# Decayed attention feeding a GELU MLP on one core: loads two chunks further ahead, and group 2's attention visits moved to later MLP blocks

## The chip, the cores and the metric

One core of a Trainium2 chip. The time is device microseconds of one execution of the kernel. Besides the timed runs, one execution is recorded by the hardware profiler; its span (first to last instruction) is shorter than its time by what lies before and after.

## The reference

q, k and v are `[4, 8, 768, 64]` float32 (batch, head, position, head dimension). The attention is causal with a decay `lam` per head and no softmax. Cut to what matters (D is the causal mask of decay powers, and the kernel uses blocks of 128 positions for the same result):

```
for each block of positions:
    intra  = ((qb @ kb.T) * D) @ vb
    inter  = (qb * lam_pow) @ kv_state
    out    = intra + inter
    kv_state = lam_block * kv_state + (kb * rev_pow).T @ vb
x = out as [3072, 512]
result = gelu(x @ w_in) @ w_out        # w_in 512 x 2048, w_out 2048 x 512, exact GELU
```

## The kernel before, in words

**Tiling.** The 3072 tokens are cut into 24 chunks of 128 positions. Chunk n belongs to batch n % 4 and to position block n // 4. Four chunks with the same position block form a group: group g holds chunks 4g to 4g+3, and there are six groups, 0 to 5. For a group the MLP runs as a list of blocks on TensorE (`mlp_blocks`): 16 blocks of `x @ w_in` (L263, four matmuls each, then a GELU on ScalarE at L265), then the blocks of `g @ w_out` (L275, four matmuls each; an output tile of 128 tokens is finished every fourth block, copied by ScalarE at L280 and written by SP at L281). In a middle group that makes 32 blocks.

**Interleaving.** The attention of group g+1 is done between the MLP blocks of group g. The dictionary `visits` says which function runs ahead of block i of group g. For chunks 8 and later, a chunk goes through these steps:

- `load` (L64 to L66): three DMAs issued by GpSimd (POOL), one each for k, q and v, from float32 in DRAM to bf16 in SBUF. Each name has a pool of 12 tiles.
- `request` (L366): `dma_transposes` (L184). SP transposes k into kT by a DMA (L188); POOL multiplies q by the decay powers into `q_hat` (L189); SP transposes `q_hat` into qT by a DMA (L190).
- `decay_k` (L165): POOL multiplies k by decay powers into `k_dec` (L169).
- `pair_a` (L411): `scores` of two chunks on TensorE, kT against qT (L197), then VectorE masks them (L201).
- `quad_b` (L415): `inter` and `intra` of the four chunks on TensorE (L224, L230), then VectorE copies the result to `x_t` (L236), the MLP's next input.
- `kv` (L378): the state update of four chunks (L209 on TensorE, L216 and L217 on VectorE).

**Who sets the order.** Each engine runs its own instructions strictly in the order in which the program issued them. The visits therefore fix the order on POOL and SP, but not the time: POOL and SP run ahead of TensorE as far as their semaphores let them. `requests(n)` is POOL's and SP's part for two chunks: two `request`, two `decay_k`, and last the loads of chunks to come (`prefetch`, L372, which issues every load not yet issued up to its argument). So on POOL the products of one pair, then six loads, then the products of the next pair follow one another. `first_requests` (L383) does chunks 8 and 9 and loads 10 and 11.

**The visits concerned.** For the groups 1 to 4 the block numbers stand in one line (L435), `a0` and `a1` for the two `pair_a`, `b` for `quad_b`, `st` for `kv`:

```
for g in range(1, NG - 1):
    n = (g + 1) * M
    a0, a1, b, st = (10, 21, 26, 31) if g == 1 else (4, 11, 18, 25)
    if g == 1:
        add(g, a0 - 2, lambda n=n: requests(n + 2))
    add(g, a0, lambda n=n: pair_a(n))
    add(g, a1, lambda n=n: pair_a(n + 2))
    if g + 2 < NG:
        add(g, a1 + 1, lambda n=n: requests(n + M))
        add(g, b + 1, lambda n=n: requests(n + M + 2))
```

Group 1 therefore requests chunks 10 and 11 (block 8), 12 and 13 (block 22), and 14 and 15 (block 27). Group 2 visits TensorE with the pairs 12, 13 (block 4) and 14, 15 (block 11), and requests 16, 17 (block 12) and 18, 19 (block 19).

Of the kernel before, what the change touches and what calls it, by code (L numbers as in the profile page):

```python
# [15 lines left out]
def kernel(  # L16
# [23 lines left out]
    M = B  # L40
# [23 lines left out]
    def load(n, name):  # L64
        raw[n, name] = qkv_pool.tile([128, H, D], BF16, tag=name, name=f"{name}_t")
        nc.gpsimd.dma_start(raw[n, name], chunk_of(name, n))  # L66
# [98 lines left out]
    def decay_k(c, eng):  # L165

        if c.so < NB - 1:
            c.k_dec = work_pool.tile([128, H, D], BF16, tag="kd", name="k_dec", bufs=8)
            eng.tensor_mul(c.k_dec, c.k, lam_m[:, :, None].to_broadcast((128, H, D)))  # L169
# [196 lines left out]
    def request(n):  # L366
        begin(n)
        dma_transposes(live[n])
# [3 lines left out]
    def prefetch(upto):  # L372
        while next_load[0] <= min(upto, NCH - 1):
            for name in "kqv":
                load(next_load[0], name)
            next_load[0] += 1

    def kv(*ns):  # L378
        for n in ns:
            next_state(live[n])  # L380
            take_state(live[n])
# [29 lines left out]
    def pair_a(n):  # L411
        for c in (live[n], live[n + 1]):
            scores(c)

    def quad_b(n):  # L415
        quad = [live[n + i] for i in range(M)]
        for c in quad:
            inter(c)
        for c in quad:
            intra(c)  # L420

    def requests(n):
        for m in (n, n + 1):
            request(m)
        for m in (n, n + 1):
            decay_k(live[m], nc.gpsimd)
        prefetch(n + 3)

    def add(g, i, f):
        visits.setdefault((g, i), []).append(f)  # L430


    for g in range(1, NG - 1):
        n = (g + 1) * M
        a0, a1, b, st = (10, 21, 26, 31) if g == 1 else (4, 11, 18, 25)  # L435
        if g == 1:
            add(g, a0 - 2, lambda n=n: requests(n + 2))
        add(g, a0, lambda n=n: pair_a(n))
# [4 lines that stand above are left out]
        add(g, b, lambda n=n: quad_b(n))  # L443
        add(g, st, lambda n=n: kv(n, n + 1, n + 2, n + 3))
# [37 lines left out]
```

## Time and profile before

| what | value |
|---|---|
| median of 6 runs | 215.26 us (213.48 to 218.02) |
| profiled execution | 216.23 us, its span 214.4 us |
| PE (TensorE matmuls) busy | 204.2 us, 95% of the span |
| POOL busy | 101.8 us, all of it ahead of 144 us |
| ACT, DVE busy | 87.2 us, 76.1 us |
| TensorE clock granted | 0.999 |
| k, q and v loads | 71 DMAs by POOL, median 5.2 to 5.9 us from issue to landing |
| kT and qT transposes | 16 and 16 DMAs by SP, median 4.7 and 3.1 us to landing |

A row of the timeline or of the chain gives a start, a duration, an engine with a line of the kernel, and what was written from what; brackets at its end give the idle time before it and what ended it. POOL and SP rows with DMA in them are the issue of a transfer; its landing is given apart, by the view of one tile ("DMA to landing"). Groups of MLP blocks are recognised by their lines: L263 for the first half, L275 for the second. By the stretches of TensorE's timeline, group 2 begins at 86.65 us, group 3 at 120.6, group 4 at 152.5 and group 5 at 183.5.

### The profile page before, as it was taken

To read this page: it belongs to the slowest core of one execution; us is meant where nothing else is said; L and a number is where in the kernel's file an instruction comes from. 1 tells how busy PE (TensorE), PEld (TensorE's weight loads), DVE (VectorE), ACT (ScalarE), POOL (GpSimd) and SP (SyncE) were. 2 spreads that over 40 slices of the span, in tenths; PEclk is the share of its full clock that TensorE was granted. 3 is DMA by queue.
4 is the path that set the end of the run, shared out by engine and by line. 5 is a ranking of instruction groups with operands and counts; after the bars stand their busy time and mean duration, and the time that the engine had idled before them with its cause. 6 is when DMAs were issued, how large, how long until landed. Compare 5 with 4: busy or idle time off the path is not lost.

```text
span 214.4 us, 3549 instructions
## 1 busy us (share of the span) xinstructions
PE 204.2 (95%) x1450; PEld 105.2 (49%) x1474; DVE 76.1 (35%) x122; ACT 87.2 (41%) x153; POOL 101.8 (47%) x117
## 2 busy tenths in 40 slices
PE   7997999999999999996999999999999999999994
PEld 2543654456654465443545444645444644444442
DVE  3777040164393234944046344037244130000000
ACT  5662654325656211553311356312365312566121
POOL 7992433792996965939697684930000000000000
PEclk9999999999999999999999999999999999999999
DMA  8999999999999699996979999993200012100112
GB/s 86 139 145 190 206 207 187 154 213 140 171 88 121 72 154 119 124 146 139 151 98 126 113 243 143 127 151 117 98 0 0 3 49 87 59 3 0 49 49 98
DMA packets 100271, 24.48 MB, mean 114 GB/s; under 512 B 92960, under 2 KB 97312, under 8 KB 100256
## 3 DMA queue, kind: packets, MB, share of 16 engines
q0 software_dynamic: 78064, 13.51, 84.3%
q1 hardware_dynamic: 22192, 10.76, 25.8%
q8 instruction: 11, 0.18, 0.4%
q14 instruction: 4, 0.03, 0.1%
HBM read 27.27 MB, written 6.29 MB: 156 GB/s over the span
## 4 chain that ended last, share of the span: by engine, by line
PE 52%; POOL 20%; DMA 20%; issue 7%; ACT 0%; POOLq 0%
PE o_ps L275 24%; PE h_ps L263 21%; DMA w_out_t<-in_moe_w_out_dram 9%; DMA q_t<-in_q_dram 6%; POOL k_dec L169 5%; POOL k_t L66 5%; POOL q_t L66 4%; DMA w_in_t<-in_moe_w_in_dram 4%; POOL v_t L66 4%; POOL q_hat L189 2%; PE o_ps L289 2%; PE o_ps L230 1%; PE o_ps L224 1%; PE sc_ps L197 1%; DMA qT<-q_hat 1%
## 5 line engine op out<-in xcount | busy, mean ns | idle before, releaser
L263 PE MATMUL h_ps<-x_t,w_in_t 128*128 128x512 bf16 (+2 forms) x422 | 86.0, 355 | 1.9 <-DMA w_in_t<-in_moe_w_in_dram 1.3
L275 PE MATMUL o_ps<-w_out_t,g_t 128*128 128x512 bf16 x356 | 81.1, 379 | 1.3 <-issue 1.0
L265 ACT ACTIVATE g_t<-h_ps 128x512 bf16<-128x512 f32 (+1 forms) x99 | 57.8, 584 | 38.3 <-PE h_ps L263 38.1
L263 PEld LDWEIGHTS <-w_in_t 128*128 128x128 bf16 x432 | 39.3, 98 | 43.1 <-DMA w_in_t<-in_moe_w_in_dram 2.2
L275 PEld LDWEIGHTS <-g_t 128*128 128x128 bf16 x368 | 35.1, 98 | 40.9
L280 ACT COPY o_sb<-o_ps 128x512 f32<-128x512 f32 x23 | 13.5, 586 | 72.6 <-PE o_ps L275 69.7
L201 DVE TENSOR_TENSOR sc_m<-sc_ps,dmask 128x512 bf16<-128x512 f32 x48 | 30.1, 683 | 35.5 <-PE sc_ps L197 35.5
L189 POOL TENSOR_TENSOR q_hat<-q_t,lam_p 128x512 bf16<-128x512 bf16 x16 | 16.8, 1052 | 24.8 <-DMA q_t<-in_q_dram 13.6
L66 POOL DMA_DIRECT2D k_t<-in_k_dram x24 | 22.0, 918 | 6.8 <-DMA w_in_t<-in_moe_w_in_dram 4.3
L66 POOL DMA_DIRECT2D q_t<-in_q_dram x24 | 21.6, 898 | 3.4 <-DMA w_out_t<-in_moe_w_out_dram 3.3
L66 POOL DMA_DIRECT2D v_t<-in_v_dram x23 | 20.8, 905 | 4.0 <-DMA w_out_t<-in_moe_w_out_dram 1.7
L236 DVE CAST x_t<-o_ps 128x512 bf16<-128x512 f32 x16 | 9.9, 684 | 19.9 <-PE o_ps L230 19.9
L169 POOL TENSOR_TENSOR k_dec<-k_t,lam_m 128x512 bf16<-128x512 bf16 x16 | 16.4, 1050 | 0.0
L216 DVE TENSOR_TENSOR tmp<-kv_ps,state 128x512 f32<-128x512 f32 x16 | 10.9, 684 | 15.0 <-PE kv_ps L209 15.0
L324 PE MATMUL idle_ps<-idle 128*128 128x512 bf16 x32 | 11.2, 465 | 1.2 <-DVE idle L105 1.2
L217 DVE TENSOR_TENSOR state<-tmp,lam_blk 128x512 bf16<-128x512 f32 x16 | 12.1, 756 | 0.6
L182 DVE TENSOR_TENSOR qT<-t_ps,lam_q 128x512 bf16<-128x512 bf16 x8 | 5.5, 691 | 14.5 <-PE t_ps L176 14.3
L197 PE MATMUL sc_ps<-qT,kT 64*128 64x128 bf16 x192 | 8.2, 217 | 2.5 <-DMA qT<-q_hat 1.8
L197 PEld LDWEIGHTS <-kT 64*128 64x128 bf16 x192 | 5.7, 94 | 8.1 <-issue 5.3
L230 PE MATMUL o_ps<-sc_m,v_t 128*64 128x128 bf16 x192 | 7.9, 222 | 0.2
L230 PEld LDWEIGHTS <-v_t 128*64 128x64 bf16 x192 | 5.8, 109 | 2.8 <-issue 1.6
L181 ACT COPY kT<-t_ps 128x512 bf16<-128x512 bf16 x8 | 4.7, 586 | 4.7 <-PE t_ps L176 4.7
(41 smaller groups left out, 70.1 us busy)
## 6 DMA issues: line engine op xcount, KB each, us to landing
out_dram<-o_sb SPq DMA_DIRECT2D x23, 256.0 KB, 2.2
k_t<-in_k_dram POOLq DMA_DIRECT2D x24, 128.0 KB, 5.2
q_t<-in_q_dram POOLq DMA_DIRECT2D x24, 128.0 KB, 5.9
v_t<-in_v_dram POOLq DMA_DIRECT2D x23, 128.0 KB, 5.8
w_in_t<-in_moe_w_in_dram POOLq DMA_DIRECT2D x4, 512.0 KB, 11.3
w_out_t<-in_moe_w_out_dram POOLq DMA_DIRECT2D x4, 512.0 KB, 18.2
v_f<-in_v_dram SPq DMA_DIRECT2D x1, 256.0 KB, 3.5
kT<-k_t SPq DMA_TRANSPOSE x16, 4.7
```

The costliest lines, as they stand in the source:

```text
L66: nc.gpsimd.dma_start(raw[n, name], chunk_of(name, n))
L169: eng.tensor_mul(c.k_dec, c.k, lam_m[:, :, None].to_broadcast((128, H, D)))
L189: nc.gpsimd.tensor_mul(q_hat, c.q, lam_p[:, :, None].to_broadcast((128, H, D)))
L197: nc.tensor.matmul(sc_ps[hi][:, hp, :], c.kT[p, hp, :], c.qT[p, hp, :], start=True, stop=True)
L201: nc.vector.tensor_mul(c.sc_m[:, :, hi, :], sc_ps[hi], dmask_r[:, :, hi, :])
L217: nc.vector.tensor_mul(new, tmp, lam_blk)
L230: nc.tensor.matmul(c.o_ps[hi * D:(hi + 1) * D, hp, :], c.v[:, 2 * hp + hi, :], c.sc_m[:, hp, hi, :], start=(c.so == 0 and hp == 0), stop=T ...
L263: nc.tensor.matmul(h_ps[:, f, :], w, x_t[:, ki, lo:hi], start=(ki == 0 and f == 0), stop=(ki == NK1 - 1), skip_group_check=True)
L265: nc.scalar.activation(g_t[:, kf:kf + n_kf, lo:hi], h_ps, ACT.Gelu)
L275: nc.tensor.matmul(om[io], g_t[:, kf, io * C:(io + 1) * C], w_out_t[:, kf, :], start=(kf == 0), stop=(kf == NK2 - 1))
L280: nc.scalar.copy(o_sb, om[io])
L324: nc.tensor.matmul(idle_ps[0], idle[:, :128], idle, start=True, stop=True)
```

## The change

Two edits. In `requests`, the loads at the end go two chunks further, with one exception: the first call (n = 10) goes one further. And group 2 gets visit numbers of its own.

```
@@ requests(n)
         for m in (n, n + 1):
             decay_k(live[m], nc.gpsimd)
-        prefetch(n + 3)
+        prefetch(n + (4 if n == 2 * M + 2 else 5))
@@ visits of the groups 1 to 4
         n = (g + 1) * M
-        a0, a1, b, st = (10, 21, 26, 31) if g == 1 else (4, 11, 18, 25)
+        a0, a1, b, st = {1: (10, 21, 26, 31), 2: (5, 15, 21, 27)}.get(g, (4, 11, 18, 25))
```

What each call of `requests` loads:

| call | before | after |
|---|---|---|
| chunks 10, 11 | 12, 13 | 12, 13, 14 |
| chunks 12, 13 | 14, 15 | 15, 16, 17 |
| chunks 14, 15 | 16, 17 | 18, 19 |
| chunks 16, 17 | 18, 19 | 20, 21 |
| chunks 18, 19 | 20, 21 | 22, 23 |
| chunks 20, 21 | 22, 23 | none |
| chunks 22, 23 | none | none |

In group 2, `pair_a(12)` moves from block 4 to 5, `pair_a(14)` from 11 to 15, `requests(16)` from 12 to 16, `quad_b(12)` from 18 to 21, `requests(18)` from 19 to 22 and `kv` from 25 to 27. The number of instructions on the engines is the same. The order of PE, DVE and POOL changes as told; on SP the write of group 2's first output tile comes ahead of the transposes of chunks 18 and 19 instead of after them.

More of the change, by code (lines that the diff above doesn't have):

```diff
@@ L426, in requests @@
             decay_k(live[m], nc.gpsimd)
-        prefetch(n + 3)
+        prefetch(n + (4 if n == 2 * M + 2 else 5))
     def add(g, i, f):
@@ L434 @@
         n = (g + 1) * M
-        a0, a1, b, st = (10, 21, 26, 31) if g == 1 else (4, 11, 18, 25)
+        a0, a1, b, st = {1: (10, 21, 26, 31), 2: (5, 15, 21, 27)}.get(g, (4, 11, 18, 25))
         if g == 1:
```

## The prediction

> **What bounds the kernel now.** I read part 1 of the page, the waits of PE, the timeline of PE, then POOL's and SP's timelines with the landing of single DMAs. PE is busy for 204.2 of 214.4 us. Its waits name one long stop after the start-up; the others that the view names (0.2 to 1.3 us) lie in the start-up or between two matmuls:
>
> ```profile
> PE sc_ps L197 <- DMA qT<-q_hat: 1.8, 1, 1.8
> ```
>
> PE's timeline shows where it is. Columns: start, length, engine, line, what, and in brackets the idle time before it.
>
> ```profile
> 97.10 0.40 PE L197 MATMUL sc_ps<-qT,kT 64*128 64x128 bf16 x8
> 99.29 0.40 PE L197 MATMUL sc_ps<-qT,kT 64*128 64x128 bf16 x8 [1.79 <-DMA qT<-q_hat]
> ```
>
> This is pair_a(14) at block 11 of group 2: chunk 14's scores ran, chunk 15's waited for its qT. Undisturbed pairs take 0.55 us on the chain; this one ended at 97.10 + 0.55 + 1.97 = 99.62. The stages agree: busy time by windows gives group 2 (86.7 to 120.6) 33.9 us and group 3 (120.6 to 152.5) 31.9 us for 222 matmuls each. So the place holds 1.97 us and no more; all later MLP groups are limited by TensorE's own work.
>
> Why is qT(15) late? POOL's timeline:
>
> ```profile
> 83.84 2.04 POOL L169 TENSOR_TENSOR k_dec<-k_t,lam_m 128x512 bf16<-128x512 bf16 x2
> 85.83 0.94 POOL L66 DMA_DIRECT2D k_t<-in_k_dram  x1
> 86.77 0.88 POOL L66 DMA_DIRECT2D q_t<-in_q_dram  x1
> 87.63 0.91 POOL L66 DMA_DIRECT2D v_t<-in_v_dram  x1
> 88.51 0.90 POOL L66 DMA_DIRECT2D k_t<-in_k_dram  x1
> 89.38 0.91 POOL L66 DMA_DIRECT2D q_t<-in_q_dram  x1
> 90.24 0.92 POOL L66 DMA_DIRECT2D v_t<-in_v_dram  x1
> 91.31 1.04 POOL L189 TENSOR_TENSOR q_hat<-q_t,lam_p 128x512 bf16<-128x512 bf16 x1
> 95.67 1.04 POOL L189 TENSOR_TENSOR q_hat<-q_t,lam_p 128x512 bf16<-128x512 bf16 x1 [3.32 <-DMA q_t<-in_q_dram]
> ```
>
> Six loads (chunks 14, 15) are issued, and the next instruction is a product that needs them. q(15), issued at 89.38, lands 6.2 us later; POOL stands 3.32 us for it. Then SP issues the transpose at 96.74, and by the view of that one tile it lands after
>
> ```profile
> DMA to landing us min/median/max: 2.4/2.4/2.4
> ```
>
> that is at 99.16. The same loads-then-wait repeats for each pair (the bracket of chunk 13's q_hat at 82.84 says 3.50).
>
> **What the Trainium skill says.** "Perfetto Trace Analysis", section "DMA Instruction — SWDGE (GPSIMD)": the recorded end of a GpSimd-issued DMA is the end of writing descriptors, not of moving data. The trace agrees: 0.88 to 0.94 us a row, and from 72 us on 3.4 to 7.9 us to landing. "DMA: Bandwidth & Descriptors", section "Issuing engines are not separate DMA queues": DMAs of SP and GpSimd run on the same 16 engines and interleave. The trace agrees: with kT(12) in flight, v(12) lands at 79.1 and k(13) at 81.8, 2.7 us apart, where loads by themselves land 0.9 apart (k16 to q17: 103.7, 104.5, 105.4, 106.2, 106.9). Same page, section "Queues, rings and completion order": an engine alternates between the queues that have work, packet by packet, which would let a transpose through soon. The trace shows less than that: kT(12), issued at 75.74 behind five loads, lands at 82.8, together with q(13), the last load issued before it; kT(14), qT(16) and qT(18) also land within 0.9 us of the last load ahead. I therefore reckon a transpose as landing behind every load issued before it, and never under 2.4 us.
>
> **The change part by part.**
>
> *Loads 14 moved into the first call.* POOL's burst at 72.17 becomes nine loads at 0.885 each, (91.14 − 85.83)/6: it ends at 80.1, not 77.5. Behind it on POOL stands q_hat(12), at 80.2 instead of 78.30; SP's qT(12) goes from 79.37 to 81.3, kT(13) behind it to 82.6, and qT(13), which still waits for q(13) at 82.8 and q_hat(13), stays at about 83.9. But v(14) is now ahead of these transposes and lands at 84.5 (v13) plus three loads, about 87.5 to 88; the transposes follow at about 0.55 us each (kT18, qT18, kT19: 120.0, 120.7, 121.2), so qT(13) lands at about 89.5 instead of 86.4. Its user, pair_a(12) at block 5, comes at 90.40 + 0.86 = 91.26. Cost: nothing, hidden by some 1.8 us; if the landing takes 7 us as kT(12) did, still 0.3 us of cover.
>
> *Nine loads (15, 16, 17) in the second call.* Issued from 85.9 to 93.8. In the built program each load waits on a semaphore shared with the load eight before it; for v(17), the last, that is k(15), due near 90 and wanted at 92.9: no stall. q_hat(14) starts at 93.95 (before 91.31), q_hat(15) directly after it at 95.0 (before 95.67), since q(15), now second of the nine, is there by about 92. POOL's 3.32 us wait is gone and 2.65 us of load issues have taken its place. On SP the order is fixed: qT(14) at 95.0, kT(15) at 96.3, qT(15) at 97.6 (1.3 apart, as at 105.68, 106.96, 108.28). So **qT(15) is issued 0.9 us later than before**; what was gained on q(15) SP's queue gives back. And it is no longer alone: loads 16 and 17 are ahead of it. The six bursts from 72 to 144 us, first to last landing, take 8.8, 6.7, 4.6, 6.7, 5.1 and 5.4 us for five intervals each, 1.24 us a load with their transposes included. From v(13) at 84.5, twelve loads give v(17) at 99.4, and three transposes at 0.55 give qT(15) at 101.05.
>
> *The later visit.* pair_a(14) at block 15 comes four blocks later than 97.10; a block is 13.82/16 = 0.864 us (group 5's L263 stretch, 183.48 to 197.30), so it starts at 100.56 and wants qT(15) at 100.84. It starts 0.13 after the landing (99.16 to 99.29), at 101.18: a stall of 0.35.
>
> *What follows.* quad_b at block 21 starts 6 blocks after block 15, 106.1 or a little later; sc_m of the pair takes 2.5 us and is done by 104. kv at block 27 is at about 113.2, and needs the score banks that the copy to x_t gives back by 111. Its VectorE work (5.5 us, as 114.16 to 119.7) ends near 119.2; pair_a(16) takes those banks at about 122. Loads 18 to 23 are earlier than before, whose users had no wait already. Tiles suffice: the loads of chunk 20 take those of chunk 8, done with at the kv of group 1 (86 us). kT(18) now stands behind an output write of SP, at about 106; it is wanted past 128. All at no cost.
>
> *Sum:* −1.97 + 0.35 = −1.62. Span 214.4 − 1.6 = 212.8, profiled execution 216.23 − 1.6 = 214.6. The median is 0.97 below the profiled execution: 213.6, 0.75% faster.
>
> **The rivals.**
>
> *The stall only moves (half or less of the gain).* qT(15) lands between 101.7 and 102.7 since loads and transposes run at burst 2's and 4's rate (6.7/5 = 1.34 us): v(17) at 100.6, qT(15) at 102.2, stall 1.5, net −0.5: 214.8. For it: two of the six bursts. Against: 16 loads in a row landed from 40.6 to 54.6 at 0.93 us each.
>
> *Slower: the queue of loads becomes the bound.* One mechanism: a transpose waits out all loads ahead of it, and there are always some now. It decides against the change when qT(15) lands after 102.7, that is when the twelve loads take over 1.38 us each. At burst 1's 8.8/5 = 1.76 they end at 105.6, qT(15) at 107.3, stall 6.6, net +4.6; halfway, at 1.5, net +1.5, 216.7. For it: burst 1 is the place where the change puts more loads, and one write of outputs and three transposes fall between. Against: that burst had the output write in its first interval (k12 to q12, 2.5 us).
>
> *It does nothing to the ordinary run.* The profiled run is slower than the median, and the fastest, 213.48, is 2.75 us below it: the 1.97 may be smaller elsewhere. Then 215.0.
>
> **How the numbers follow.** Forecast (gain of 1 us or more) 0.58: 213.6. Stall moves 0.2: 214.8. Does nothing 0.08: 215.0. Slower 0.14: 216.7. The range reaches from 212.4 (the whole 1.97 plus a sampling of 0.9 us, the runs being spread over 4.5) to 216.4, most of the slower case; the likeliest case alone has 213.0 to 214.3. A measurement of this kernel can tell about 1% from no change, 2.15 us. The gain cannot be over 1.97, so faster by over 1% needs luck in the sampling: 0.15. Slower by over 1% is the upper half of the slower case: 0.08. Within: 0.77.
>
> **What would show it.** Group 2 in 32 to 32.4 us; PE's stop at L197 gone or under 0.5 us and no new one at pair_a(12); nine loads in a row on POOL twice; no bracket on the q_hat of chunk 15; qT(13) landing near 89.5, qT(15) issued near 97.6 and landing near 101. I am wrong if qT(15) lands past 102, if a load waits for the one eight before it and holds q_hat(14) back, or if PE stops near 91.

## The result, and the profile after

The changed kernel took 215.52 us (median of 36 runs, 213.28 to 218.92) against 214.85 us (73 runs) of the kernel before. The ratio is 1.0021 with a 95% interval of 1.0004 to 1.0037, taken over undisturbed runs alone, which leaves out six of the changed kernel with a granted clock of 0.991 to 0.992. The kernel became a little slower, and the forecast gain of 0.75% did not come.

The profiled execution took 216.2 us, span 214.4 us. In the waits of PE the same line is there, and longer:

```profile
PE sc_ps L197 <- DMA qT<-q_hat: 2.2, 1, 2.2
```

PE's timeline (start, length, what, idle time before it) shows it at the same pair, now at block 15:

```profile
100.09 0.40 PE L197 MATMUL sc_ps<-qT,kT 64*128 64x128 bf16 x8
102.72 0.40 PE L197 MATMUL sc_ps<-qT,kT 64*128 64x128 bf16 x8 [2.23 <-DMA qT<-q_hat]
103.05 1.04 PE L263 MATMUL h_ps<-x_t,w_in_t 128*128 128x512 bf16 x4
```

The pair comes 3.0 us later than before (100.09 against 97.10) and still waits. Undisturbed it would have ended at 100.09 + 0.55 = 100.64; the next block starts at 103.05, so the place costs 2.41 us, where it cost 1.97. By the starts of L263 in PE's timeline group 2 now lasts from 86.39 to 120.64, 34.25 us, against 86.85 to 120.67, 33.82 us: 0.43 us more, or 0.2%. That this is also the ratio of the ordinary runs is in part luck, since the stop is not equally long in every execution (see below). (The spans are equal because group 2 began 0.46 us earlier in this execution.)

POOL's timeline around the second burst, the middle of it left out:

```profile
82.62 2.04 POOL L169 TENSOR_TENSOR k_dec<-k_t,lam_m 128x512 bf16<-128x512 bf16 x2
84.61 0.94 POOL L66 DMA_DIRECT2D k_t<-in_k_dram  x1
...
91.61 0.94 POOL L66 DMA_DIRECT2D v_t<-in_v_dram  x1
92.50 2.12 POOL L189 TENSOR_TENSOR q_hat<-q_t,lam_p 128x512 bf16<-128x512 bf16 x2
94.51 2.10 POOL L169 TENSOR_TENSOR k_dec<-k_t,lam_m 128x512 bf16<-128x512 bf16 x2
96.49 0.94 POOL L66 DMA_DIRECT2D k_t<-in_k_dram  x1
97.43 0.88 POOL L66 DMA_DIRECT2D q_t<-in_q_dram  x1
98.30 0.90 POOL L66 DMA_DIRECT2D v_t<-in_v_dram  x1
```

Nine loads run from 84.61 to 92.5, and the two q_hat of chunks 14 and 15 follow as one row with no bracket: the 3.32 us wait is gone. POOL therefore reaches the loads of chunk 18 at 96.49. Before, the next loads (of chunk 16) came at 98.66, 1.92 us behind the issue of qT(15) at 96.74; POOL's and SP's rows of before:

```profile
96.67 2.04 POOL L169 TENSOR_TENSOR k_dec<-k_t,lam_m 128x512 bf16<-128x512 bf16 x2
98.66 0.94 POOL L66 DMA_DIRECT2D k_t<-in_k_dram  x1
```

```profile
96.74 1.19 SPq L190 DMA_TRANSPOSE qT<-q_hat  x1
```

SP's timeline after the change, and the landing of its last transpose:

```profile
93.65 1.19 SPq L190 DMA_TRANSPOSE qT<-q_hat  x1
94.93 2.28 SPq L188 DMA_TRANSPOSE kT<-k_t  x1
97.31 1.21 SPq L190 DMA_TRANSPOSE qT<-q_hat  x1
```

```profile
DMA to landing us min/median/max: 5.3/5.3/5.3
```

qT(15) is issued at 97.31, near the 97.6 forecast, but takes 5.3 us to land, at 102.6; before it was 2.4. When its issue ends, at 98.52, POOL has already issued k(18) and q(18).

### The profile page after: what moved, and what is told of

The parts are those of the page before. It is cut to its first block, busy times and chain, and to the rows that moved or that the text cites. A ratio compares the mean times of both kernels' runs of the same rounds, so it can differ in the third digit from the quotient of the medians.

```text
span 214.4 us, 3545 instructions
## 1 busy us (share of the span) xinstructions
PE 204.0 (95%) x1449; PEld 105.5 (49%) x1474; DVE 76.1 (35%) x122; ACT 87.3 (41%) x153; POOL 101.9 (48%) x117
## 4 chain that ended last, share of the span: by engine, by line
PE 84%; DMA 6%; POOL 5%; issue 2%; SPq 1%; ACT 0%; POOLq 0%
PE o_ps L275 37%; PE h_ps L263 35%; DMA w_in_t<-in_moe_w_in_dram 4%; PE o_ps L230 3%; PE sc_ps L197 2%; DMA qT<-q_hat 2%; PE kv_ps L209 2%; PE o_ps L224 2%; POOL k_t L66 2%; PE o_ps L289 2%; POOL q_t L66 2%; POOL v_t L66 1%; SPq L188 1%; POOL q_hat L189 1%; PE t_ps L176 1%
## 5 line engine op out<-in xcount | busy, mean ns | idle before, releaser
L263 PE MATMUL h_ps<-x_t,w_in_t 128*128 128x512 bf16 (+2 forms) x422 | 85.8, 355 | 1.6 <-DMA w_in_t<-in_moe_w_in_dram 1.0
L263 PEld LDWEIGHTS <-w_in_t 128*128 128x128 bf16 x432 | 39.3, 98 | 42.6 <-DMA w_in_t<-in_moe_w_in_dram 1.5
L189 POOL TENSOR_TENSOR q_hat<-q_t,lam_p 128x512 bf16<-128x512 bf16 x16 | 17.3, 1107 | 9.2 <-DMA q_t<-in_q_dram 7.4
L197 PE MATMUL sc_ps<-qT,kT 64*128 64x128 bf16 x192 | 8.2, 217 | 2.9 <-DMA qT<-q_hat 2.2
L197 PEld LDWEIGHTS <-kT 64*128 64x128 bf16 x192 | 5.7, 94 | 8.5 <-issue 6.2
```

Source lines behind the costliest of these rows:

```text
L189: nc.gpsimd.tensor_mul(q_hat, c.q, lam_p[:, :, None].to_broadcast((128, H, D)))
L197: nc.tensor.matmul(sc_ps[hi][:, hp, :], c.kT[p, hp, :], c.qT[p, hp, :], start=True, stop=True)
L263: nc.tensor.matmul(h_ps[:, f, :], w, x_t[:, ki, lo:hi], start=(ki == 0 and f == 0), stop=(ki == NK1 - 1), skip_group_check=True)
```

## The experiments

In what follows "stop" is the idle time of PE at L197 in pair_a(14), in the profile of that run. Landings are those of single DMAs, asked one by one in the view by tile.

**The visits alone.** The loads of before, the visits after:

```
-        a0, a1, b, st = (10, 21, 26, 31) if g == 1 else (4, 11, 18, 25)
+        a0, a1, b, st = {1: (10, 21, 26, 31), 2: (5, 15, 21, 27)}.get(g, (4, 11, 18, 25))
```

> The changed visits of group 2 with the loads of the kernel before. Theory (the gain of the later visit is real and the loads eat it): POOL and SP run as before, qT(15) is issued near 96.7 and lands near 99.2, the pair at block 15 wants it near 100.5, so PE does not stop at L197 in group 2; group 2 falls from 33.9 to about 32.0 us, ratio 0.991 (0.988 to 0.994). Rival (the later visits themselves cost what the stop gave, or the ordinary run has no such stop): ratio 0.998 to 1.003.

Measured: 0.9966 (0.9939 to 0.9993), span of the profile 212.4. qT(15) was issued at 95.37, landed at 97.8, and the pair ran as one row of 16 without a bracket:

```profile
100.46 0.62 PE L197 MATMUL sc_ps<-qT,kT 64*128 64x128 bf16 x16
```

So the later visit by itself takes the stop away, as the theory said, but it is worth less in the ordinary run: 0.34% in place of 0.9%.

**The loads alone.** The visits of before, the loads after:

```
-        prefetch(n + 3)
+        prefetch(n + (4 if n == 2 * M + 2 else 5))
```

> The changed loads with the visits of the kernel before, so pair_a(14) is back at block 11. Theory (the loads make qT(15) late): it lands as in the changed kernel, 102 to 103, against a pair that wants it at about 97.4: a stop of 4.5 to 5.5 us, 2.7 to 3.5 more than before, ratio 1.012 to 1.017. Rival (the landing follows TensorE's visit and not the queues): a stop of about 2 us as in both kernels, ratio 1.000.

Measured: 1.0191 (1.0137 to 1.0244), over six runs whose granted clock was 0.984 to 0.991 in each. PE stops twice at the pair, 3.84 us together:

```profile
97.66 0.40 PE L197 MATMUL sc_ps<-qT,kT 64*128 64x128 bf16 x8 [1.04 <-DMA qT<-q_hat]
100.86 0.50 PE L197 MATMUL sc_ps<-qT,kT 64*128 64x128 bf16 x8 [2.80 <-DMA qT<-q_hat]
101.29 6.03 PE L263 MATMUL h_ps<-x_t,w_in_t 128*128 128x512 bf16 x20
```

The stop is somewhat shorter than expected, the time somewhat longer, because the clock drops after it: 20 matmuls take 6.03 us where before they took 4.49:

```profile
99.62 4.49 PE L263 MATMUL h_ps<-x_t,w_in_t 128*128 128x512 bf16 x20
```

The windows of that stretch (busy time and count by engine, then the granted clock as a share of full speed, DMA share and GB/s) show it in the second row:

```profile
97.00:101.00 4.00, 0.54 (x14) 0.43 (x16) 1.29 (x2) 0.26 (x1) 4.00 (x6) 1.00 0.91 132
101.00:104.00 3.00, 3.00 (x15) 1.13 (x12) 1.29 (x2) 0.60 (x1) 3.00 (x4) 0.50 1.41 189
```

The loads alone are thus a loss of about 1.9%, the lower clock included, and the rival (the landing follows the visit) is out. In the whole change the later visit covers the greater part of what the loads do.

**Loads 18 and 19 held back.** The changed kernel, with nothing loaded at the end of the call for chunks 14 and 15; the nine loads stay:

```
-        prefetch(n + (4 if n == 2 * M + 2 else 5))
+        prefetch(n + {2 * M + 2: 4, 3 * M + 2: 3}.get(n, 5))
```

> The changed kernel, but loads 18 and 19 are not issued at the end of the call for chunks 14 and 15; the next call issues 18 to 21. The nine loads 15, 16, 17 stay. Theory A (qT(15) waits behind loads 18, which POOL now issues ahead of it): qT(15), issued near 97.3, lands 2.4 to 3 us later, near 100; stop under 0.3 us, ratio 0.991. Theory B (the burst of nine loads itself holds it): it lands at 101.5 or later as in the changed kernel (102.6), stop 1.3 us or more, ratio 0.997 to 1.002.

Measured: 0.9939 (0.991 to 0.9967), span 211.7, no stop. SP, and the landing of the last of the three:

```profile
93.18 1.19 SPq L190 DMA_TRANSPOSE qT<-q_hat  x1
94.47 1.22 SPq L188 DMA_TRANSPOSE kT<-k_t  x1
95.79 1.93 SPq L190 DMA_TRANSPOSE qT<-q_hat  x1
```

```profile
DMA to landing us min/median/max: 4.1/4.1/4.1
```

It lands at 99.9, 1.6 us behind v(17) at 98.3. The burst of nine by itself (Theory B) does not make the pair late here; what follows it does (Theory A). The cover is thin, though: in two later profiles with 18 and 19 held back, stops of 0.27 and 1.20 us were left (the table below has them).

**k first on SP.** The changed kernel, with SP's order for this pair kT(14), kT(15), qT(14), qT(15). Cut to the new lines of `requests`; the two functions are `dma_transposes` taken apart:

```
+        if n == 3 * M + 2:
+            for m in (n, n + 1):
+                transpose_k(live[m])
+            for m in (n, n + 1):
+                transpose_q(live[m])
```

> The changed kernel, but SP issues the two k transposes of the pair 14, 15 ahead of its two q transposes; POOL's order is untouched. Theory (qT(15) is issued too late on SP, behind kT(15), and so behind loads 18): qT(15) is issued near 95 instead of 97.3, ahead of all loads of chunk 18, and lands behind v(17), at 98.5 to 99.5; no stop, ratio 0.991. Rival (the engines are too full whatever the place in the queue, 5.3 us a transpose and more for the last of four): it lands after 101, stop 0.7 us or more, ratio 0.995 to 1.000.

Measured: 0.9972 (0.9948 to 0.9995). In its profile POOL's burst began 1.5 us later than in the changed kernel (86.10), v(17) landed at 100.6, qT(14) at 101.1 and qT(15), issued at 97.2 and so ahead of k(18) (97.98), at 101.8: 1.2 us behind v(17), two stops of 0.76 and 0.29 us. I had expected a landing at 98.5 to 99.5; the rival's landing came in, but with its transpose right behind v(17), as in the run before and not as in the changed kernel. It helps, and the place of kT(15) on SP is a part of the delay.

**One chunk further ahead, early and late visit.** `prefetch(n + 4)` in all calls, which puts six loads instead of nine ahead of the products of 14 and 15; once with the visits of before, once with the changed ones.

> The kernel before with every call loading one chunk further ahead instead of two, and the visits of before. POOL then has the loads 12, 13, 14, the products of 12, 13, the loads 15, 16, the products of 14, 15, the loads 17, 18. Theory (what counts is how many loads POOL puts between the products of one pair and the next, and ahead of the pair's transposes): POOL's 3.3 us wait for q(15) is gone with six loads ahead of its product instead of nine, so qT(15) is issued near 93.6 and lands at 96 to 97.3, against a pair that wants it at about 97.3; stop under 0.5 us, ratio 0.992 to 0.996. Rival (any load further ahead makes the transposes late): qT(15) lands after 98.5, stop 1.3 us or more, ratio 0.999 or more.

> One chunk further ahead, with the changed visits of group 2. Both theories: no stop, since the visit is 3.4 us later still; what is left is TensorE's own work, ratio 0.993 to 0.995, as with loads 18 and 19 held back (0.9939). If it is clearly below that, something else than the stop was gained.

Measured: 0.9988 (0.9962 to 1.0014) and 0.9998 (0.9977 to 1.002), neither clear of no change, and both misses against 0.992 to 0.996 and 0.993 to 0.995. The profiles bear out the place: with the early visit qT(15) was issued at 93.12 and landed at 96.4, and the pair ran at 96.61 without a stop. With the late visit there was none at pair_a(14) either, but one in group 1, at pair_a(10), whose visit no edit touches:

```profile
73.79 0.40 PE L197 MATMUL sc_ps<-qT,kT 64*128 64x128 bf16 x8 [1.11 <-DMA qT<-q_hat]
```

The pattern of pair_a(14) stands there again, without a burst ahead: k(12) was issued at 70.38, 0.20 us behind qT(11) (70.18), and qT(11) took 3.5 us to land. In the profile with the early visit k(12) came 1.40 us behind it (70.62 and 69.22), and it took 2.4.

**Loads 19 alone held back.** In the changed kernel, `prefetch(n + 4)` in the call for chunks 14 and 15.

> The changed kernel, but of loads 18 and 19 only those of chunk 18 follow the products of chunks 14 and 15. Theory (order: only what is issued ahead of qT(15) delays it, and that is k(18) and q(18)): as in the changed kernel, qT(15) lands at 101.3 to 102.7, stop 1 to 2.3 us, ratio 0.998 to 1.003. Rival (volume: what is in the engines while the transpose moves, issued after it too): half the loads, half the delay: it lands near 101, stop 0.3 to 0.8 us, ratio 0.995 to 0.997.

Measured: 1.0024 (1.0002 to 1.0047), as the changed kernel. qT(15), issued at 96.47, landed at 101.2:

```profile
101.28 0.40 PE L197 MATMUL sc_ps<-qT,kT 64*128 64x128 bf16 x8 [1.63 <-DMA qT<-q_hat]
```

Taking half of the loads away gave nothing; the half that was left has k(18) and q(18) issued ahead of qT(15), at 95.45 and 96.38. The landing is near the 101 of the rival of volume, but the stop and the time are twice and more what it allowed, so it is out.

**The pair two blocks earlier.** The kernel before with `a1 = 9` in group 2.

> The kernel before with pair_a(14) at block 9 of group 2 instead of 11; POOL and SP issue the same in the same order. The stop must grow by two blocks, 1.73 us, to about 3.5 us. Theory A (a stop of that length also lowers TensorE's clock for some 3 us, as a window of the loads-only run shows after 2.8 us: 0.50): 1.6 us on top, 3.3 in all, ratio 1.013 to 1.018. Theory B (the stop costs its own length): ratio 1.006 to 1.010, clock 1.0 throughout.

Measured: 1.0108 (1.0036 to 1.018), too wide to part the two theories. The profiled execution had a stop of 2.11 us only:

```profile
94.69 0.40 PE L197 MATMUL sc_ps<-qT,kT 64*128 64x128 bf16 x8
97.19 0.40 PE L197 MATMUL sc_ps<-qT,kT 64*128 64x128 bf16 x8 [2.11 <-DMA qT<-q_hat]
```

qT(15) landed at 97.1 there, against 99.16 in the profile before, with the same instructions on POOL and SP. At block 11, 1.73 us later, that execution would have stopped for about 0.4 us, by this estimate. So the 1.97 us of the profile before is probably not what every execution has. Of the six runs two had clock 1.0 and took 215.9 and 216.3 us, four had 0.984 to 0.992 and took 218.7 to 221.7: this agrees with Theory A without proving its price.

**All on one chip.** The changed kernel, the one with 18 and 19 held back, the same with pair_a(10) moved too, and the one-ahead late kernel, side by side. The edit of the third:

```
-{1: (10, 21, 26, 31), 2: (5, 15, 21, 27)}
+{1: (10, 23, 27, 32), 2: (5, 15, 21, 27)}
```

> The changed kernel itself, on one chip with the three that follow. All theories: ratio 0.999 to 1.005 as measured before, a stop of 1.5 to 2.5 us at pair_a(14).

> The changed kernel with loads 18 and 19 held back, unchanged, on another chip. Theory (holding them back takes the stop at pair_a(14) away): no stop there, 0.4 to 0.9% below the changed kernel on the same chip. Rival (its 0.9939 was the chip or the sample): level with the changed kernel within 0.2%.

> As the one before, and group 1 visits with pair_a(10) at block 23 instead of 21 (quad_b at 27, kv at 32); POOL and SP keep their order. In the profile of one kernel PE stopped 1.11 us at pair_a(10), where qT(11) has only 0.6 us to spare in the profile before. Theory (that stop is in a part of all runs and is why an ordinary run gives back less than the 1.97 us of the profile): a further 0.1 to 0.4%, and no stop at L197 in groups 1 and 2. Rival (that stop is rare): level with the run before within 0.1%.

> One chunk further ahead with the changed visits again, now beside the run that holds 18 and 19 back. Theory (neither has a stop at pair_a(14), what differed was the chip and the runs): level with it within 0.3%. Rival (loading 17 and 18 behind the products of 14, 15 still costs something): 0.4% or more above it, and a stop at pair_a(14).

Measured, each against the kernel before on that chip: 1.0049 (1.002 to 1.0079), 0.9973 (0.9949 to 0.9996), 0.9975 (0.9954 to 0.9997), 0.9966 (0.9943 to 0.999). PE's timeline of the first two at the second half of the pair:

```profile
101.95 0.40 PE L197 MATMUL sc_ps<-qT,kT 64*128 64x128 bf16 x8 [1.82 <-DMA qT<-q_hat]
```

```profile
100.63 0.40 PE L197 MATMUL sc_ps<-qT,kT 64*128 64x128 bf16 x8 [0.27 <-DMA qT<-q_hat]
```

Holding the loads back is worth 1.0049 − 0.9973 = 0.76%, 1.6 us, on one chip, and that is 1.55 us by the two stops, though a stop of 0.27 us was left where none was expected. The rival of the second run (its 0.9939 was the chip or the sample) falls as to the gain; the size, 0.27% here, was smaller. In the third the theory falls: moving pair_a(10) gave nothing, so the stop there is rare, or the later visits cost as much. In the fourth the theory stands: the one-ahead kernel is level with the held one, so the chip or the sample is the likely reason of its 0.9998.

## Why the prediction was wrong, point by point

*What bounds it:* right. One stop on TensorE's path, at pair_a(14); in the changed profile nothing else of the change moved TensorE.

*Loads 14 in the first call, at no cost:* right. qT(13) was issued at 83.64 and landed at 86.9, earlier than the 89.5 reckoned, and pair_a(12) ran at 90.80 without a stop.

*Nine loads in the second call:* the order and the end of POOL's wait were right; POOL was 1.1 to 1.6 us earlier than reckoned throughout. v(17) landed at 97.8, not 99.4, and that was luck: the count began earlier, with v(13) at 82.4 in place of 84.5. The twelve loads themselves took (97.8 − 82.4)/12 = 1.28 us each, slightly more than the 1.24 reckoned. No load waited for the one eight before it.

*The step that failed* is the end of that sum, "three transposes at 0.55 give qT(15) at 101.05": it counts the loads ahead of qT(15) up to v(17) and leaves out the next ones, 18, which the same edit brings forward on POOL. Under "What follows" it did count loads 18 to 23 as earlier, but asked only about their own users and put them "at no cost". It noted that POOL's 3.32 us wait for q(15) goes away and did not ask what else that wait had been doing. The wait let SP issue qT(14) and kT(15) meanwhile, so that qT(15) went out as soon as its product was done, with two products of POOL still ahead of the next loads: the 1.92 us of before. Without it the two products of q end together, SP's three transposes queue up, and POOL goes on. By the prediction's own figures q_hat(15) ends at 96.05, two k_dec take 2.04, and k(18) is issued at 98.1, half a microsecond behind qT(15) at 97.6; measured, it was 0.82 us ahead (0.22 behind in the other profile of the changed kernel). The runs show the term with its two values:

| kernel | v(17) lands | qT(15) issued | k(18) issued | qT(15) lands | behind v(17) | stop |
|---|---|---|---|---|---|---|
| changed | 97.8 | 97.31 | 96.49 | 102.6 | 4.7 | 2.23 |
| changed again | 98.2 | 98.05 | 98.27 | 101.8 | 3.6 | 1.82 |
| loads alone | 96.9 | 96.89 | 97.13 | 100.7 | 3.8 | 1.04 + 2.80 |
| 19 held back | 97.3 | 96.47 | 95.45 | 101.2 | 3.9 | 1.63 |
| k first | 100.6 | 97.2 | 97.98 | 101.8 | 1.2 | 0.76 + 0.29 |
| 18, 19 held back | 98.3 | 95.79 | 100.86 | 99.9 | 1.6 | none |
| held back again | 98.9 | 97.35 | 101.24 | 100.5 | 1.6 | 0.27 |
| held back, pair 10 later | 100.6 | 99.11 | 102.95 | 102.1 | 1.5 | 0.63 + 0.57 |

With the next loads 3 us or more behind, the last transpose lands 1.5 to 1.6 us after v(17), which is the 1.65 us of the prediction. With k(18) issued no later than 0.3 us after qT(15) begins to be issued, it is 3.6 to 4.7. In the changed profile that is 3.1 us too much, of which v(17), 1.6 us earlier than reckoned, hid half; the pair itself came 0.5 us earlier too (100.09 for 100.56). So −1.97 + 0.35 was forecast, and −1.97 + 2.41 came. The prediction's own sign of being wrong, qT(15) past 102, is there.

The second rival ("there are always some now") had the right mechanism, with the wrong place for its price: it needed over 1.38 us for each of the twelve loads, and they took 1.28. The first rival (the stall only moves) had the landing in its range, 101.7 to 102.7, but by slower loads, so by luck.

*The long issue of kT(15)*, 2.28 us on SP in the changed profile, is not the cause: in the changed kernel's other profile it took 1.22 us and the stop was there; in the held kernel's second profile it took 1.95 and the stop was 0.27.

*The size in ordinary runs:* the kernels without a stop at the pair, or with a short one, gain 0.0 to 0.6% and not 0.9%. The likely reason is that the stop in the profile before was a long one (by the estimate above, 0.4 us would have been left in the execution of "two blocks earlier"); how long it is in ordinary runs was not measured. So the third rival, which had 0.08, holds in part.

*Still open:* whether loads 18 delay qT(15) by standing ahead of it in the engines or by sharing them while it moves. The rule of the prediction (a transpose lands behind every load issued before it) is not exact: in the changed kernel's second profile and in the loads-alone run, k(18) was begun 0.2 us after qT(15), and qT(15) landed 1.3 to 1.5 us ahead of k(18), and still 2 us late.

How close behind loads must follow to do harm is open too. In "k first" 0.8 us behind did little; at pair_a(10) 0.2 us was enough and 1.4 us did nothing. But in the two one-ahead profiles with the late visit k(17) was issued 2.0 and 0.9 us behind qT(15), which landed 2.9 and 3.1 us after v(16), the last load ahead of it (1.7 and 1.5 us with the early visit). And in the visits-alone profile qT(14) landed 1.9 us after v(15), when no later load had been issued yet. Loads close behind bring the delay, as the runs that take them away show; they do not account for every late transpose.

*The section "Queues, rings and completion order"* of the page "DMA: Bandwidth & Descriptors" of the Trainium skill says that an engine alternates between its queues packet by packet. That fits a transpose which is slowed by loads issued 0.2 us behind it, and lands ahead of them, better than my rule does; no view here shows the packets themselves.

## What to carry to other kernels

When an edit takes a wait off an engine that also issues DMAs, list what that engine will issue sooner, and look for a transfer that lived from the quiet which the wait made. A prefetch that is early enough should be put behind the last transfer that someone waits for, not just ahead of its own use: here the same loads, issued one call later, turned a loss of 0.2 to 0.5% into a gain of 0.3 to 0.6%. Test the two halves of such a change apart, since a later visit can hide most of what earlier loads cost. Here the later visit alone gave 0.34%, as much as most of the kernels that also load further ahead; no run shows a gain of the loads themselves (one chunk ahead alone: 0.9988, not clear of no change).

## What the runs showed of the hardware that was not expected

After PE had been idle for 3.84 of 4.24 us (two stops with 0.40 us of work between), its granted clock was 0.50 from 101.02 to 104.43 us and 1.00 from there to 108, and the stop cost about 1.5 us more than its length (6.03 against 4.49 us for 20 matmuls); after stops of 2.23 and 2.11 us in the profiles of the changed kernel and of "two blocks earlier" the clock stayed at 1.0. The Trainium skill, "TensorE: Matmul & The Clock Gate", section "What's actually happening", gives half the clock after about one idle window of 3.4 us, which agrees, with the addition that 0.40 us of matmuls inside the stretch did not prevent it. Over all executions whose clock is on record, a mean of 0.992 or less stands beside 39 of 258 of the kernels whose profile has a stop of 1.6 us or more at pair_a(14), and beside 1 of 154 of those with none or under 0.8 us. That the stop is what lowers it was seen in one profile alone, that of the loads.

A transpose issued by SP took 2.4 us to land where it was least disturbed (qT(15) before); among loads it took up to 9.2 us in the changed profile (kT(16), issued at 99.71, landed at 108.9).
